# Summing the first quad's exponentials on GpSimd before TensorE takes the softmax sums

## The chip, the cores and the metric

One core of a Trainium2 chip runs the whole kernel. The metric is the device time of one execution in microseconds (us). Engines are named as in the profile: PE is TensorE, PEld its weight loads, DVE is VectorE, ACT is ScalarE, POOL is GpSimd, SP is SyncE.

## The reference

```python
scores = scale * np.matmul(q, k.transpose(0, 1, 3, 2))      # batch 8, 12 heads, 448 rows, head_dim 64
scores = scores - np.max(scores, axis=-1, keepdims=True)
attn = np.exp(scores)
attn = attn / (np.sum(attn, axis=-1, keepdims=True) + 1e-09)
x = (attn @ v)  -> [3584, 768]
h = x @ w_in                                                 # 768 x 2048
out = (h * np.cos(h)) @ w_out                                # 2048 x 768
```

## The kernel before

Four heads make a quad, a batch has three quads (c = 0, 1, 2), and the 448 keys of a quad are handled in seven chunks (r). A planning clock in Python estimates when each engine is free, lays down the order of all instructions ahead of time and gives each engine its own list in that order. The parts that matter:

```python
# S: scores of one chunk on PE, exponential on ACT
nc.scalar.activation(out=pT[b, c][:, r, :, :], in_=sc[:, :, 0:S_], func=AF.Exp, scale=scale)

# DN: sums over keys, on PE, into den (four matmuls, each on 32 columns of its own)
for c in cs:
    for r in rs:                      # seven chunks
        for h in range(2):
            for qh_ in range(2):
                nc.tensor.matmul(den[b][32 * g : 32 * g + 32, :], onehot[:, c, :],
                                 pT[b, c][:, r, h, ts(qh_, SH)], ...)

# N: reciprocal and six small copies on DVE
nc.vector.reciprocal(out=rr[:, 0], in_=den[b])
# ... six copies of 32 rows ...

# M: per quad, two shuffles and one product with two SBUF inputs, on DVE
nc.vector.stream_shuffle(out=rb[:, j], in_=..., mask=[row] * 32)      # j = 0, 1
nc.vector.tensor_tensor(out=xT[b, c], in0=asb[b, c], in1=rb, op=ALU.mult)

# H: the projection to 2048 takes xT quad by quad (hps), then cos on ACT and gT on DVE
# O: the projection back (ops); PE uses it to fill waits in attention and behind den
```

A quad's attention output is copied from PSUM, where this kernel's matmuls put their results, into `asb`; `rb` holds the reciprocals of the sums, spread over the rows by the shuffles; `xT` is their product, the scaled heads. At the end of a batch PE runs `den`, the last `av` and two to five score chunks of the next batch, then `ops` as filler until N and M have made xT.

The softmax here doesn't subtract the row's maximum and nothing guards it: scores larger than these inputs give would overflow.

Of the kernel before, what the change touches and what calls it, by code (L numbers as in the profile page):

```python
# [11 lines left out]
FP = mybir.dt.float32  # L12
F16 = mybir.dt.float16
AF = mybir.ActivationFunctionType
ALU = mybir.AluOpType


class Clock:
# [3 lines left out]


    def __init__(self, slots):
        self.pe = self.act = self.dve = self.stall = 0.0
        self.mode = self.table = None
        self.slots = {k: [0.0] * n for k, n in slots.items()}
        self.ready = {}

    def copy(self):  # L30
        c = Clock({})
        c.pe, c.act, c.dve, c.stall = self.pe, self.act, self.dve, self.stall
        c.mode, c.table = self.mode, self.table
        c.slots = {k: list(v) for k, v in self.slots.items()}
        c.ready = dict(self.ready)
        return c
# [22 lines left out]
    def on_act(self, dep, dur, table=None):  # L59
        if table is not None and table != self.table:  # L60
            self.act += 1.3
            self.table = table
        self.act = max(self.act, dep) + dur
        return self.act + 0.15

    def on_dve(self, dep, dur):
        self.dve = max(self.dve, dep) + dur
# [4 lines left out]
def kernel(  # L72
# [9 lines left out]
    nc = tc.nc  # L82

    B, NH, S_, D = q.shape
    E = moe_w_in.shape[0]
    F = moe_w_in.shape[1]
    P = 128
    NR = 7
    SP = S_ // NR
    NQ = NH // 4  # L90
# [8 lines left out]
    const = ctx.enter_context(tc.tile_pool(name="const", bufs=1))  # L99
    wpool = ctx.enter_context(tc.tile_pool(name="wpool", bufs=1))  # L100
    ld = ctx.enter_context(tc.tile_pool(name="ld", bufs=3))
    sb = ctx.enter_context(tc.tile_pool(name="sb", bufs=2))
    big = ctx.enter_context(tc.tile_pool(name="big", bufs=1))
# [1 line left out]



    clk = Clock({"big": 3, "m": 2, "pT": 4, "qkp": 3, "qkT": 4, "asb": 4, "xT": 3, "gT": 2})


    def quad_rows(t):
# [53 lines left out]

    ident = const.tile([P, P], F16, name="ident")
    onehot = const.tile([P, NQ, 32], F16, name="onehot")
    lowrow = const.tile([P, 1], FP, name="lowrow")
    ind = []
    halfpi = const.tile([P, 1], FP, name="halfpi")  # L170
# [3 lines left out]
    def emit_consts_vector():  # L174
        nc.vector.memset(zero, 0.0)


        nc.vector.memset(onehot, 0.0)
        nc.vector.memset(onehot[:, 0, 2 * NQ : 16], 1.0)
        nc.vector.memset(onehot[:, 0, 16 + 2 * NQ :], 1.0)  # L180
        for j in range(2):
            for half in range(2):
                for c in range(NQ):
                    m = 16 * half + 2 * c + j
                    nc.vector.memset(onehot[64 * j : 64 * j + 64, c, m : m + 1], 1.0)
        nc.vector.memset(halfpi, math.pi / 2)

    def emit_consts_late():

# [25 lines left out]
    pairs, qkT, pT, asb, den, rrs, rhl, xT, gT = ({} for _ in range(9))  # L215
# [151 lines left out]
    def AV(ck, b, c, rs=range(NR)):  # L367
        ck.need(max(ck.ready.get(("pT", b, c, rs[-1]), LATER), arrive["v", b, c]))
        first, last = rs[0] == 0, rs[-1] == NR - 1
        if first:  # L370
            ck.ready["av slot", b, c], t = take(ck, "big", None if b else (2,))
            ck.need(t)
        at = ck.ready["av slot", b, c]
        end = ck.mm("quarters", len(rs), 0.189)
        if last:
            ck.ready["asb slot", b, c], t = take(ck, "asb", None)
            on, took = (ck.on_act, 0.92) if c == NQ - 1 else (ck.on_dve, 1.09)
            ck.slots["big"][at] = ck.ready["asb", b, c] = on(max(end, t), took)
        if ck is not clk:
            return  # L380
        p = pT[b, c]
        vn = nat["v", b, c]
        if first:
            avs[c] = ps.tile([P, 2, 512], FP, name="av", tag=f"big{at}")
        for r in rs:
            for j in range(2):
                for h in range(2):
                    nc.tensor.matmul(  # L388
                        avs[c][64 * h : 64 * h + 64, j, 0:S_],
                        vn[64 * j : 64 * j + 64, h, ts(r, D)],  # L390
                        p[64 * j : 64 * j + 64, r, h, :],
                        start=(r == 0),
                        stop=(r == NR - 1),
                    )
        if not last:
            return
        a = sb.tile([P, 2, S_], FP, name="asb", tag=f"asb{ck.ready['asb slot', b, c]}", bufs=1)
        asb[b, c] = a
        copy = nc.scalar.copy if c == NQ - 1 else nc.vector.tensor_copy
        copy(out=a, in_=avs[c][:, :, 0:S_])  # L400
        emit_load_v()
        if b == 0 and c == 2:
            emit_w_out(1)
            for _ in held_back[1:]:
                emit_load_qk()
            held_back.clear()

    def AVS(ck, b, c, b2, chunks):

        AV(ck, b, c)  # L410
        S(ck, b2, chunks)

    def DN(ck, b, cs, rs=range(NR)):


        ck.need(ck.ready.get(("pT", b, cs[-1], rs[-1]), LATER))
        if cs[0] == rs[0] == 0:
            ck.ready["den slot", b], t = take(ck, "m", None)
            ck.need(t)
        for c in cs:  # L420
            ck.ready["den", b] = end = ck.mm("col32", len(rs), 0.0935)
            if rs[-1] == NR - 1:
                ck.slots["pT"][ck.ready["pT slot", b, c]] = end
        if ck is not clk:
            return
        if cs[0] == rs[0] == 0:
            den[b] = ps.tile([P, SH], FP, name="den", tag=f"m{ck.ready['den slot', b]}")
        for c in cs:
            for r in rs:
                for h in range(2):  # L430
                    for qh_ in range(2):
                        g = 2 * qh_ + h if b < BY_SHUFFLE else 2 * h + qh_
                        nc.tensor.matmul(  # L433
                            den[b][32 * g : 32 * g + 32, :],
                            onehot[:, c, :],
                            pT[b, c][:, r, h, ts(qh_, SH)],
                            start=(c == 0 and r == 0),
                            stop=(c == NQ - 1 and r == NR - 1),
                        )
# [226 lines left out]
    def run(step):  # L666
        step[0](clk, *step[1:])
# [4 lines left out]
    def transpose_ahead():  # L672

        while to_transpose:
            b, c = to_transpose[0]
            now = max(clk.pe, clk.dve)
            if zeros and b > 0:
                return
            if arrive.get(("qk", b, c), LATER) > now - (1.0 if b and c else 0.0) or min(clk.slots["qkp"]) > now or min(clk.slots["qkT"]) > now:
                return  # L680
            to_transpose.pop(0)
            run((W, b, c))
            if (b, c) > BY_PE:
                run((X, b, c))
            else:
                soon.extend([(T, b, c, i) for i in ((0, 1) if b + c == 0 else (1, 0))])

    def weave(lists, keep, late=99):



        body = lists[0]
        while body:
            transpose_ahead()
            waits = []
            todos = ([body, soon] if opening else [soon, body])
            due = stall(body[0]) if opening else 1e9
            for todo in todos + (lists[1:] if len(body) <= late else []):
                while todo and todo[0][0] in (N, M):
                    run(todo.pop(0))  # L700
                if todo:
                    w, took = cost(todo[0])
                    if todo is not body and took > due + 0.15:
                        continue
                    if w <= SLACK:
                        run(todo.pop(0))
                        break
                    waits.append((w, todo))
            else:
                least = min(waits, key=lambda x: x[0])[0] if waits else 1e9  # L710
                if len(fill) > keep or fill and least > 0.3:
                    waits.append((stall(fill[0]), fill))
                    least = min(least, waits[-1][0])
                if zeros and least > 0.15 and due > 0.15:
                    run((Z,))
                elif least > 1e6:
                    clk.pe += 0.1
                else:
                    run(min(waits, key=lambda x: x[0])[1].pop(0))
# [32 lines left out]
    LATER = 1e9  # L752
    SLACK = 0.02
    QUIET = 5
    BY_PE = (2, 0)
    AHEAD, LATE, KEEP = 1, 6, 8
    ctx.enter_context(tc.manual_schedule(engines=None))
# [39 lines left out]
    values = values[:-8] + [step for step in values[-8:] if step[0] is DN] + [(N, 0)] + late  # L797
    last = scores[-QUIET:]
    weave([scores[:-QUIET], values], 0)
    zeros.clear()  # L800
# [4 lines left out]
    body = []  # L805
    for b in range(B):
# [13 lines left out]
        body = ahead + nxt[AHEAD if b else 4 :]  # L820
# [32 lines left out]
```

## Time and profile before

| | before |
|---|---|
| median time | 415.05 us (3 runs, 414.9 to 415.1) |
| span of the profiled run | 413.1 us |
| PE busy, idle | 405.0, 8.1 us |
| POOL busy | 68.6 us, 62.8 of it issuing loads |
| `den` | 672 matmuls, 84 a batch in 2.13 us, 25.4 ns each |
| xT product on DVE | 21 of 1.092 us |

A group's row on the page has the line of code, engine, operation, output and inputs, count, then busy time and mean length of one in ns, then the engine's idle time ahead of the group and what ended most of it. The chain of waits and the order of time give start, length, engine and what. The lines themselves stand in the prediction.

### The profile page before, as it was taken

How to read it: one execution, taken by the hardware profiler on the slowest of the kernel's cores; microseconds unless marked ns; L12 is line 12 of the kernel's file. 1: busy time of each engine (PE TensorE's matmuls, PEld its weight loads, DVE VectorE, ACT ScalarE, POOL GpSimd, SP SyncE). 2: the span in 40 equal slices, each digit the busy share in tenths (PEclk: the TensorE clock that was granted, in tenths of full speed). 3: DMA queues.
4: the chain of work that ended last, by engine and by line, in shares of the span. 5: the costliest groups of instructions: out<-in, count | busy, mean ns of one | idle time of the engine just before them, and what ended most of it. 6: DMA issues, size and time to landing. Idle time of an engine off the chain costs nothing.

```text
span 413.1 us, 8921 instructions
## 1 busy us (share of the span) xinstructions
PE 405.0 (98%) x3835; PEld 217.9 (53%) x3835; DVE 202.7 (49%) x356; ACT 250.2 (61%) x299; POOL 68.6 (17%) x103
## 2 busy tenths in 40 slices
PE   8989999999999999899999999999999999999996
PEld 3445546555565555555565555655556555555564
DVE  3365634945247443754429443575426643294400
ACT  5986386656756478544867457574685547734311
POOL 7687204200320023000230003100000000000000
PEclk9999999999999999999999999999999999999999
DMA  9999999992995039950898009950473101210033
GB/s 191 190 152 201 204 212 200 147 133 63 167 175 108 2 56 174 139 103 2 144 162 146 21 19 110 180 119 2 83 108 78 26 0 40 53 45 2 19 76 79
DMA packets 67239, 42.65 MB, mean 103 GB/s; under 512 B 34304, under 2 KB 67200, under 8 KB 67200
## 3 DMA queue, kind: packets, MB, share of 16 engines
q0 software_dynamic: 26496, 22.35, 38.8%
q1 hardware_dynamic: 40256, 19.18, 26.9%
q8 instruction: 30, 0.49, 0.6%
q10 hardware_dynamic: 448, 0.56, 0.4%
q14 instruction: 9, 0.07, 0.1%
HBM read 45.61 MB, written 11.01 MB: 137 GB/s over the span
## 4 chain that ended last, share of the span: by engine, by line
PE 89%; DMA 4%; DVE 2%; ACT 1%; POOL 1%; issue 1%; POOLq 0%; DVEq 0%
PE ops L635 35%; PE hps L582 34%; PE sc L352 7%; PE av L388 7%; PE den L433 4%; DMA win<-in_moe_w_in_dram 2%; DMA vn<-in_v_dram 2%; DVE rb L482 1%; PE tp L307 1%; ACT pT L361 1%; POOL qkn L133 1%; DVE xT L486 1%; DVE rr L451 0%; POOL vn L143 0%; ACT qkT L319 0%
## 5 line engine op out<-in xcount | busy, mean ns | idle before, releaser
L361 ACT ACTIVATE pT<-sc 128x896 f16<-128x896 f32 x168 | 142.4, 921 | 20.3 <-PE sc L352 20.2
L582 PE MATMUL hps<-xT,win 128*128 128x448 f16 x768 | 149.4, 352 | 0.1
L635 PE MATMUL ops<-wout,gT 128*128 128x384 f16 x768 | 137.5, 327 | 1.3 <-issue 1.3
L592 ACT ACTIVATE cs<-hps,halfpi 128x896 f32<-128x896 f32 x64 | 63.6, 1007 | 79.5 <-PE hps L582 76.7
L582 PEld LDWEIGHTS <-win 128*128 128x128 f16 x768 | 74.8, 98 | 69.2 <-issue 0.9
L593 DVE TENSOR_TENSOR gT<-cs,hps 128x896 f16<-128x896 f32 x64 | 68.9, 1087 | 72.4 <-ACT cs L592 72.3
L635 PEld LDWEIGHTS <-gT 128*128 128x128 f16 x768 | 70.6, 98 | 62.5 <-issue 19.4
L352 PE MATMUL sc<-qkT 64*64 64x448 f16 x672 | 46.9, 357 | 0.7 <-ACT pT L361 0.4
L133 POOL DMA_DIRECT2D qkn<-in_q_dram x23 | 16.6, 722 | 134.4 <-DVE qkp L245 131.3
L388 PE MATMUL av<-pT,vn 64*64 64x448 f16 x672 | 38.0, 353 | 0.3 <-DMA win<-in_moe_w_in_dram 0.3
L400 DVE COPY asb<-av 128x896 f32<-128x896 f32 x16 | 17.5, 1091 | 34.0 <-PE av L388 34.0
L143 POOL DMA_DIRECT2D vn<-in_v_dram x24 | 17.2, 719 | 99.9 <-PE sc L352 98.1
L645 DVE COPY osb<-ops 128x384 f32<-128x384 f32 x25 | 13.9, 556 | 37.2 <-PE ops L635 37.2
L645 ACT COPY osb<-ops 128x384 f32<-128x384 f32 (+1 forms) x32 | 15.1, 472 | 26.6 <-DMA out_dram<-osb 17.0
L352 PEld LDWEIGHTS <-qkT 64*64 64x64 f16 x672 | 17.8, 105 | 22.1 <-issue 15.7
L388 PEld LDWEIGHTS <-vn 64*64 64x64 f16 x672 | 17.7, 106 | 14.9 <-issue 6.5
L482 DVE STREAM_SHUFFLE rb<-rr 128x448 f32<-128x448 f32 x42 | 25.5, 656 | 0.1
L400 ACT COPY asb<-av 128x896 f32<-128x896 f32 x8 | 7.3, 907 | 27.9 <-PE av L388 27.9
L486 DVE TENSOR_TENSOR xT<-asb,rb 128x896 f16<-128x896 f32 x21 | 22.9, 1092 | 1.2
L635 PE MATMUL ops<-wout,rest 128*128 128x384 f16 (+1 forms) x144 | 23.2, 308 | 0.0
L451 DVE RECIPROCAL rr<-den 128x224 f32<-128x224 f32 x8 | 12.5, 1558 | 18.6 <-PE den L433 18.6
L433 PE MATMUL den<-pT,onehot 128*32 128x224 f16 x672 | 18.9, 260 | 0.0
(47 smaller groups left out, 160.7 us busy)
## 6 DMA issues: line engine op xcount, KB each, us to landing
out_dram<-osb SPq DMA_DIRECT2D x110, 96.0 KB, 2.7
vn<-in_v_dram POOLq DMA_DIRECT2D x24, 224.0 KB, 8.1
qkn<-in_q_dram POOLq DMA_DIRECT2D x23, 224.0 KB, 8.0
qkn<-in_k_dram POOLq DMA_DIRECT2D x23, 224.0 KB, 8.8
win<-in_moe_w_in_dram POOLq DMA_DIRECT2D x16, 192.0 KB, 8.4
wout<-in_moe_w_out_dram POOLq DMA_DIRECT2D x2, 1536.0 KB, 18.7
stage<-in_q_dram SPq DMA_DIRECT2D x2, 224.0 KB, 3.6
stage<-in_k_dram ACTq DMA_DIRECT2D x2, 224.0 KB, 3.8
```

The source lines that it names most:

```text
L352: nc.tensor.matmul(sc[lo, h, 0:S_], t[64 * h : 64 * h + 64, 1, r, lo], t[64 * h : 64 * h + 64, 0, :, lo], start=True, stop=True,)
L361: nc.scalar.activation(out=pT[b, c][:, r, :, :], in_=sc[:, :, 0:S_], func=AF.Exp, scale=scale)
L388: nc.tensor.matmul(avs[c][64 * h : 64 * h + 64, j, 0:S_], vn[64 * j : 64 * j + 64, h, ts(r, D)], p[64 * j : 64 * j + 64, r, h, :], start=( ...
L400: copy(out=a, in_=avs[c][:, :, 0:S_])
L433: nc.tensor.matmul(den[b][32 * g : 32 * g + 32, :], onehot[:, c, :], pT[b, c][:, r, h, ts(qh_, SH)], start=(c == 0 and r == 0), stop=(c == ...
L482: nc.vector.stream_shuffle(out=rb[:, j], in_=rrs[b].rearrange("p q s -> p (q s)"), mask=[row] * 32)
L486: nc.vector.tensor_tensor(out=xT[b, c], in0=asb[b, c], in1=rb, op=ALU.mult)
L582: nc.tensor.matmul(hpss[f2][:, i, 0:S_], w_in16[:, kc, ts(2 * f2 + i, P)], xT[b, kc // 2][:, kc % 2, :], start=(kc == 0), stop=(kc == NKC ...
L592: nc.scalar.activation(out=cos, in_=hpss[f2][:, :, 0:S_], func=AF.Sin, bias=halfpi)
L593: nc.vector.tensor_tensor(out=gT[b][:, 2 * f2 : 2 * f2 + 2, :], in0=cos, in1=hpss[f2][:, :, 0:S_], op=ALU.mult,)
L635: nc.tensor.matmul(ops, tokens, w_out16[:, fc, ds(lo, n)], start=(fc == 0), stop=(fc == NFC - 1),)
L645: (nc.scalar.copy if on_act else nc.vector.tensor_copy)(out=osb, in_=ops)
```

## The change

The sums over the seven chunks of quad 0 are first made elementwise on Pool, in FP32. The sum is then split into an FP16 part (ACT, scaled by 1/8) and the FP16 remainder (DVE), written over the first two chunks, and PE sums over partitions with a one-hot of 8. That takes five groups of four matmuls off PE in each of batches 2 to 7. One of four `asb` buffers is given up for the sum's tile. The diff, cut to its core (the planning clock's bookkeeping is left out):

```diff
-    clk = Clock({..., "asb": 4, ...})
+    clk = Clock({..., "asb": 3, ...})
+        nc.vector.tensor_scalar(out=onehot8, in0=onehot, scalar1=8.0, scalar2=None, op0=ALU.mult)
+    SUMMED, SUMMED_FROM = (0,), 2
+    def U(ck, b, c, r):
+        ...
+        if r == 1:
+            totals[b, c] = sb.tile([P, 2, S_], FP, name="sum", tag=f"sum{c}", bufs=1)
+        first = p[:, 0] if r == 1 else totals[b, c]
+        engine = nc.gpsimd if c == 0 else nc.vector
+        engine.tensor_tensor(out=totals[b, c], in0=first, in1=p[:, r], op=ALU.add)
+    def V(ck, b, c):
+        ...
+        nc.scalar.mul(out=hi, in_=totals[b, c], mul=0.125)
+        nc.vector.scalar_tensor_tensor(
+            out=lo, in0=totals[b, c], scalar=0.125, in1=hi, op0=ALU.mult, op1=ALU.subtract)
     def DN(...):
-            for r in rs:
+            for r in range(2) if c in summed else rs:
-                            onehot[:, c, :],
+                            (onehot8 if c in summed else onehot)[:, c, :],
+    def sum_ahead(due):     # emits U and V as soon as the planning clock has their inputs
```

More of the change, by code (lines that the diff above doesn't have):

```diff
@@ L24, in __init__ @@
     def __init__(self, slots):
-        self.pe = self.act = self.dve = self.stall = 0.0
+        self.pe = self.act = self.dve = self.pool = self.stall = 0.0
         self.mode = self.table = None
@@ L31, in copy @@
         c = Clock({})
-        c.pe, c.act, c.dve, c.stall = self.pe, self.act, self.dve, self.stall
+        c.pe, c.act, c.dve, c.pool, c.stall = self.pe, self.act, self.dve, self.pool, self.stall
         c.mode, c.table = self.mode, self.table
@@ L64, in on_act, with on_pool @@
         return self.act + 0.15
+    def on_pool(self, dep, dur):
+        self.pool = max(self.pool, dep) + dur
+        return self.pool + 0.15
     def on_dve(self, dep, dur):
@@ L104 @@
     ps = ctx.enter_context(tc.tile_pool(name="ps", bufs=1, space=bass.MemoryType.PSUM))
-    clk = Clock({"big": 3, "m": 2, "pT": 4, "qkp": 3, "qkT": 4, "asb": 4, "xT": 3, "gT": 2})
+    clk = Clock({"big": 3, "m": 2, "pT": 4, "qkp": 3, "qkT": 4, "asb": 3, "xT": 3, "gT": 2})
     def quad_rows(t):
@@ L167 @@
     onehot = const.tile([P, NQ, 32], F16, name="onehot")
+    onehot8 = const.tile([P, NQ, 32], F16, name="onehot8")
     lowrow = const.tile([P, 1], FP, name="lowrow")
@@ L373, in AV @@
         at = ck.ready["av slot", b, c]
-        end = ck.mm("quarters", len(rs), 0.189)
+        ck.ready["av", b, c] = end = ck.mm("quarters", len(rs), 0.189)
         if last:
@@ L411, in AVS @@
         S(ck, b2, chunks)
+    SUMMED, SUMMED_FROM = (0,), 2
+    totals = {}
+    def U(ck, b, c, r):
+        on, took = (ck.on_pool, 2.1) if c == 0 else (ck.on_dve, 1.0)
+        ck.ready["sum", b, c, r] = on(max(ck.ready["pT", b, c, i] for i in (0, r)), took)
+        if ck is not clk:
+            return
+        p = pT[b, c]
+        if r == 1:
[4 more added lines that the diff above has]
+    def V(ck, b, c):
+        t = ck.on_act(max(ck.ready["sum", b, c, NR - 1], ck.ready["av", b, c]), 0.82)
+        ck.ready["sum", b, c] = ck.on_dve(t, 1.0)
+        if ck is not clk:
+            return
+        hi, lo = (pT[b, c][:, i] for i in range(2))
+        nc.scalar.mul(out=hi, in_=totals[b, c], mul=0.125)
+        nc.vector.scalar_tensor_tensor(
+            out=lo, in0=totals[b, c], scalar=0.125, in1=hi, op0=ALU.mult, op1=ALU.subtract
+        )
     def DN(ck, b, cs, rs=range(NR)):
+        summed = [c for c in cs if b >= SUMMED_FROM and c in SUMMED]
         ck.need(ck.ready.get(("pT", b, cs[-1], rs[-1]), LATER))
+        for c in summed:
+            ck.need(ck.ready.get(("sum", b, c), LATER))
         if cs[0] == rs[0] == 0:
@@ L420, in DN @@
         for c in cs:
-            ck.ready["den", b] = end = ck.mm("col32", len(rs), 0.0935)
+            ck.ready["den", b] = end = ck.mm("col32", 2 if c in summed else len(rs), 0.0935)
             if rs[-1] == NR - 1:
@@ L686, in transpose_ahead @@
                 soon.extend([(T, b, c, i) for i in ((0, 1) if b + c == 0 else (1, 0))])
+    to_sum = {c: [] for c in SUMMED}
+    for b in range(SUMMED_FROM, B):
+        for c in SUMMED:
+            to_sum[c] += [(U, b, c, r) for r in range(1, NR)] + [(V, b, c)]
+    def sum_ahead(due):
+        for c, steps in to_sum.items():
+            while steps:
+                step = steps[0]
+                b = step[1]
+                at = clk.pool if c == 0 and step[0] is U else clk.dve
+                if step[0] is U:
+                    t = clk.ready.get(("pT", b, c, step[3]), LATER)
+                else:
+                    t = max(clk.ready.get(("sum", b, c, NR - 1), LATER), clk.ready.get(("av", b, c), LATER))
+                ready = t <= max(clk.pe, at) and at <= clk.pe + BACKLOG
+                if not ready and b > due:
+                    break
+                run(steps.pop(0))
     def weave(lists, keep, late=99):
@@ L694, in weave @@
             transpose_ahead()
+            sum_ahead(body[0][1] if body[0][0] is DN else -1)
             waits = []
@@ L754 @@
     QUIET = 5
+    BACKLOG = 1.0
     BY_PE = (2, 0)
```

## The prediction

Three things in it are my assumptions, which no trace of the kernel before shows: 2.05 us for a Pool add (the change's planning clock counts 2.1), the whole-instruction rule of case C (an add and an xT product exclude each other for the length of an instruction), and in case B that each xT is stretched by half.

> **What bounds the kernel now.** I read the page first, busy shares and groups, then the chain that ended last, then the instructions in order of time around one batch. On the page of the kernel before:
>
> ```profile
> PE 405.0 (98%) x3835; PEld 217.9 (53%) x3835; DVE 202.7 (49%) x356; ACT 250.2 (61%) x299; POOL 68.6 (17%) x103
> ...
> L486 DVE TENSOR_TENSOR xT<-asb,rb 128x896 f16<-128x896 f32 x21 | 22.9, 1092 | 1.2
> ...
> L433 PE MATMUL den<-pT,onehot 128*32 128x224 f16 x672 | 18.9, 260 | 0.0
> ```
>
> TensorE has work for 98% of the 413.1 us span, so the schedule is a list of PE work with hardly a hole, and an engine that helps is useful only while it makes PE wait for nothing new. The sums over keys (`den`) are 672 matmuls and 18.9 us busy: the only group this change shortens.
>
> The chain of waits, cut to batch 3 (165 to 217 us), shows the price of `den` and the order behind it:
>
> ```profile
> 165.60 2.13 PE den L433 x84
> 167.73 1.45 PE av L388 x28
> 169.18 0.38 PE sc L352 x8
> 169.56 2.38 PE ops L635 x14
> 171.94 0.69 PE sc L352 x12
> 172.63 0.92 PE ops L635 x5
> 173.55 1.26 issue
> 174.81 0.65 PE ops L635 x3
> 175.46 1.51 PE hps L582 x8
> 176.97 0.65 PE ops L635 x4
> 177.62 1.51 PE hps L582 x8
> 179.13 0.65 PE ops L635 x4
> 179.78 15.13 PE hps L582 x80
> ```
>
> After `den`, PE is fed with output matmuls (`ops`) until VectorE has turned den into the scaled heads xT, and the second projection (`hps`) starts on them one quad at a time. In the order of time of DVE and ACT in the same stretch the three xT products and the first exponentials of the next batch stand side by side:
>
> ```profile
> 172.48 1.09 DVE L486 TENSOR_TENSOR xT<-asb,rb 128x896 f16<-128x896 f32 x1
> ...
> 174.73 1.09 DVE L486 TENSOR_TENSOR xT<-asb,rb 128x896 f16<-128x896 f32 x1
> ...
> 177.07 1.09 DVE L486 TENSOR_TENSOR xT<-asb,rb 128x896 f16<-128x896 f32 x1
> ```
>
> ```profile
> 170.03 1.73 ACT L361 ACTIVATE pT<-sc 128x896 f16<-128x896 f32 x2
> ...
> 172.30 2.53 ACT L361 ACTIVATE pT<-sc 128x896 f16<-128x896 f32 x3 [0.17 <-PE sc L352]
> ```
>
> The last xT ends at 177.07 + 1.09 = 178.16 and PE takes up the group that needs it at 179.62 by its own timeline: 1.46 us to spare. I took the same difference in every batch whose successor will be summed on Pool (batches 1 to 6): 0.05, 0.36, 1.46, 0.36, 0.05 and 0.35 us, 2.63 us in all. That is almost nothing: these three products are nearly on PE's path.
>
> [...] The trace before has no Pool arithmetic of this kind. [...] of one of the small copies (rr, L459)
>
> ```profile
> L459 DVE COPY rr<-rr x14: 266/270/331, 74.4 to 365.0; 32x224 f32<-32x224 f32 x14
> ```
>
> the slow ones of 0.33 us are those that ran while Pool was issuing a load of v (169.95 beside the load issued at 169.50); in batch 7, which has no such load, it took 0.27. [...] The trace has 1.092 for xT; I use that for the new subtraction on DVE.
>
> **The change, part by part.** Removed: in batches 2 to 7 quad 0 takes two chunks of four matmuls instead of seven, so 6 x 5 x 4 = 120 matmuls. One group of 84 takes 2.13 us in the chain, 2.13 / 84 = 25.4 ns each[...]. So 120 x 25.4 ns = **3.04 us** of PE, all on the path, 0.73% of 415.05. This is the most the change can win by its own arithmetic.
>
> Added on Pool: 6 batches x 6 adds x 2.05 = 74 us; Pool was busy for 68.6, much of it at the opening, so it has room. In each batch its adds take 12.3 us, and the chance to do them is long: four can follow the exponentials at 170 to 175, two those of the next attention stage (the chunks from 198.4), and the sum is wanted by `den` at 214.97. Even with the two splitting steps it is ready near 207, an estimate from these starts. So den itself won't wait for Pool. Loads issued by Pool can stand behind an add for 2 to 4 us; they take a median 8 us to land and are asked for a quad or more ahead, so I give this nothing.
>
> Added on ACT: six scalings, each about 0.92 us (the asb copy of equal size takes 0.907). ACT is busy for 16.32 of the 20 us from 195 to 215, and its waits there are for PE's scores, so 0.92 fits. Added on DVE: six subtractions of 1.09, in a stage where it's busy for 7.65 of 20. Both wait for finished sums and lie off the path; 0.1 us in all for the one-time scaled one-hot. One asb buffer fewer (3 for 4): its slot is wanted again only after the xT of the batch before, so no wait.
>
> Moved: nothing by hand, but the order is laid by a planning clock, and output matmuls shift among the gaps. I take 0 plus or minus 1 us for it.
>
> **Where it can go wrong: the two engines meet.** [...] The second exponential of the next batch ends at 170.03 + 1.73 = 171.76, so the first add runs from about 171.85 to 173.9. xT 0 wants to start at 172.48, reads two SBUF tensors, and if the whole-instruction rule holds, starts at 173.9 instead (+1.42). It ends at 175.0; the second add then runs to 177.05; xT 1, wanted at 176.16 after its two shuffles, starts at 177.05 (+2.32). The third add runs from 178.14 to 180.19, and xT 2 starts there instead of 177.07 (+3.12). Against 2.63 us of slack over six batches: 6 x 3.12 - 2.63 = 16.1 us of new PE waits, less 3.0 won: +13.1, **428.1 us**.
>
> **The rivals.**
> A: no contention that counts. Then 415.05 - 3.04 with 0.2 lost on the added steps: **412.2 us**. For it: [...] the change is aimed carefully, with start batch and backlog set.
> B: [...] each xT stretched by half: 3 x 0.55 = 1.6 a batch, less 2.63 / 6 = 0.44 slack, x 6 = 7.2, less 3.0: **about 419 us**.
> C: the full lock as worked above, **428.1 us**. For it: [...] the overlap in all six batches. Against it: an add that is faster than 2.05 us shortens it quickly (at 1.6 us the same steps give +1.85 instead of +3.12, near 420).
> D: Pool late, with ACT (in order) held at the scaling, and the exponentials behind it. The window of some 8 us before den speaks against it; at 3 us an add it would begin to bite. I count it within the upper range. If Pool never let DVE in between adds, four adds in a row would cost some 8 us a batch and over 450 us; I give that under 5%.
>
> **Range and chances.** I weigh A 0.35, B 0.20, C 0.45: 0.35 x 412.2 + 0.20 x 419 + 0.45 x 428.1 = 420.7. I put 420.5; it is a mean of unlike outcomes, and the true time is more likely near 412 or above 424 than there. The range, 411.5 to 430, spans A to C. Faster by 2% means under 406.7, 8.3 us won, where 3.04 is the most on the list: 0.01. Slower by 2% is above 423.4: nearly all of C and a little of B, 0.44. The rest, 0.55, is within 2%.
>
> **What the profile after would show.** den x552 matmuls instead of 672 and near 15.5 us busy proves the gain. The mean of one Pool add says whether 2.05 holds. For C the three xT start up to 3 us later behind den than now, with DVE or Pool named between den and `hps` in the chain of waits, in batches 1 to 6 and not in 7; for A the xT keep their distances from den and PE's idle time stays near 8 us. For D, ACT's scaling would wait long for Pool. The prediction is wrong if the planner has moved the adds behind xT, or if the planning clock, with changed costs, lays down a much better or worse order.

## The result, and the profile after

The changed kernel takes **421.67 us** (4 runs, 421.6 to 421.96), the kernel before 414.98 in the same rounds. The ratio is 1.0165, 95% interval 1.0148 to 1.0183: slower, but within 2%. A ratio here is the mean time of one kernel's runs over that of the other's runs of the same rounds, so it isn't quite the ratio of the quoted medians. Executions over 1.5% slower than the fastest of the same kernel are left out of the means.

From the page of the kernel after, the engines' busy shares, the chain by engine, and three groups:

```profile
PE 405.4 (97%) x3715; PEld 214.5 (51%) x3715; DVE 218.0 (52%) x358; ACT 256.0 (61%) x310; POOL 148.4 (35%) x139
...
PE 76%; DVE 19%; ACT 1%; DMA 1%; issue 1%; ACTq 0%; DVEq 0%
...
L620 PE MATMUL hps<-xT,win 128*128 128x448 f16 x768 | 149.4, 353 | 8.3 <-DVE xT L524 8.2
...
L435 POOL TENSOR_TENSOR sum<-sum,pT 128x896 f32<-128x896 f32 x30 | 68.5, 2282 | 36.5 <-ACT pT L367 34.9
...
L524 DVE TENSOR_TENSOR xT<-asb,rb 128x896 f16<-128x896 f32 x21 | 33.1, 1574 | 1.6 <-DVE rb L520 0.5
```

PE's idle time rose from 8.1 to 14.5 us (419.9 - 405.4), and its new idle time lies before `hps` and is ended by xT. The same 21 products take 33.1 us instead of 22.9, though their code is unchanged: 10.2 us more. DVE now makes up 19% of the chain that ends last, where it was 2%.

The expected saving is there, though den is 16.0 us busy and not the 15.5 that were expected. Its group after:

```profile
L471 PE MATMUL den<-pT,onehot 128*32 128x224 f16 x552 | 16.0, 260 | 0.0
```

The chain of waits after, at batch 3, from den to the 80 long matmuls of `hps`:

```profile
168.74 1.67 PE den L471 x64
170.44 1.57 DVE rr L489
...
175.14 2.20 DVE xT L524
...
178.58 1.45 DVE xT L524
...
181.34 1.46 DVE xT L524
182.84 15.29 PE hps L620 x80
```

den is done in 1.67 us instead of 2.13. But where the chain went through PE all the way before, it now goes through DVE: three xT of 2.20, 1.45 and 1.46 us. From the end of den to the end of the third xT it was 178.16 - 167.73 = 10.43 us; now 182.80 - 170.41 = 12.39. The order of time of the same stretch shows who lies beside them:

```profile
174.58 1.87 POOL L435 TENSOR_TENSOR sum<-pT 128x896 f32<-128x896 f16 x1 [1.71 <-ACT pT L367]
175.14 2.26 DVE L524 TENSOR_TENSOR xT<-asb,rb 128x896 f16<-128x896 f32 x1
176.53 8.00 POOL L435 TENSOR_TENSOR sum<-sum,pT 128x896 f32<-128x896 f32 x3
...
177.33 0.65 DVE L520 STREAM_SHUFFLE rb<-rr 128x448 f32<-128x448 f32 x1
...
178.58 1.51 DVE L524 TENSOR_TENSOR xT<-asb,rb 128x896 f16<-128x896 f32 x1
...
181.34 1.45 DVE L524 TENSOR_TENSOR xT<-asb,rb 128x896 f16<-128x896 f32 x1
```

The two engines take turns. The first add ends at 174.58 + 1.87 = 176.45; the xT that wanted to start at 175.14 ends at 177.40, 0.95 us later. The second add, recorded from 176.53, is stretched in its turn: the three take 8.00 us with the gaps between them, some 2.6 each, against 1.87 for the first, which held the product up. The shuffles between the products have one SBUF input; they lie beside the same adds and keep their 0.65 us. Note how the profile shows the wait: the product blocked at 175.14 has no idle time ahead of it and no releaser. It only looks longer than its kind.

### The profile page after: what moved, and what is told of

It reads as the page before. It is cut to its first block, busy times and chain, and to the rows that moved or that the text cites. A ratio compares the mean times of both kernels' runs of the same rounds, so it can differ in the third digit from the quotient of the medians.

```text
span 419.9 us, 8770 instructions
## 1 busy us (share of the span) xinstructions
PE 405.4 (97%) x3715; PEld 214.5 (51%) x3715; DVE 218.0 (52%) x358; ACT 256.0 (61%) x310; POOL 148.4 (35%) x139
## 4 chain that ended last, share of the span: by engine, by line
PE 76%; DVE 19%; ACT 1%; DMA 1%; issue 1%; ACTq 0%; DVEq 0%
PE hps L620 30%; PE ops L673 27%; DVE xT L524 7%; PE sc L358 7%; DVE rb L520 6%; PE av L394 6%; PE den L471 4%; DVE rr L489 3%; PE tp L313 1%; DVE rr L497 1%; DMA stage<-in_k_dram 1%; DVE rr L496 1%; PE z L237 1%; DVE rr L495 1%; ACT pT L367 1%
## 5 line engine op out<-in xcount | busy, mean ns | idle before, releaser
L620 PE MATMUL hps<-xT,win 128*128 128x448 f16 x768 | 149.4, 353 | 8.3 <-DVE xT L524 8.2
L435 POOL TENSOR_TENSOR sum<-sum,pT 128x896 f32<-128x896 f32 x30 | 68.5, 2282 | 36.5 <-ACT pT L367 34.9
L524 DVE TENSOR_TENSOR xT<-asb,rb 128x896 f16<-128x896 f32 x21 | 33.1, 1574 | 1.6 <-DVE rb L520 0.5
L683 ACT COPY osb<-ops 128x384 f32<-128x384 f32 (+1 forms) x37 | 17.7, 477 | 24.9 <-DMA out_dram<-osb 12.8
L444 DVE SCALAR_TENSOR_TENSOR pT<-sum,pT 128x896 f16<-128x896 f32 x6 | 6.6, 1092 | 27.1 <-ACT pT L443 27.1
```

The lines of the kernel that those rows point to most:

```text
L435: engine.tensor_tensor(out=totals[b, c], in0=first, in1=p[:, r], op=ALU.add)
L620: nc.tensor.matmul(hpss[f2][:, i, 0:S_], w_in16[:, kc, ts(2 * f2 + i, P)], xT[b, kc // 2][:, kc % 2, :], start=(kc == 0), stop=(kc == NKC ...
```

## The experiments

Theory **L**: a Pool add and a DVE instruction with two SBUF inputs exclude each other for the length of an instruction, which makes xT late and PE wait. Rival **O**: the changed order of PE's work costs the time. Rival **S**: the split on ACT and DVE does.

### The adds held back behind xT

```diff
         if r == 1:
             totals[b, c] = sb.tile([P, 2, S_], FP, name="sum", ...)
+            nc.vector.memset(totals[b, c][:, 0, 0:1], 0.0)     # behind the third xT of batch b-1
```

The planning clock is told of the same wait, so that it emits the add only once xT is due. The memset of one column lies behind the third xT on DVE's list, and the add that overwrites the tile waits for it.

> The changed kernel, but each batch's first Pool add also waits, through a one-element VectorE memset of the sum's tile placed behind the third xT product of the batch before, until the three xT products are done. Correct result. Theory L (a Pool add and a VectorE product with two SBUF inputs exclude each other for a whole instruction, and the late xT makes PE wait): all 21 xT back to 1.09 us, Pool adds all near 1.88 us, PE's waits for xT gone; time of the kernel before less 6 x 0.45 us of den = about 412.3 (412 to 413.2). Rival O (the changed order of PE's work costs the time): the order is nearly that of the changed kernel, so 419 to 422. Rival S (the split on ACT and VectorE costs): 419 or more, xT at 1.09 all the same.

It is correct and takes 412.11 us (4 runs, 411.89 to 415.98; before 415.19, ratio 0.9954, interval 0.9907 to 1.0000, wide because of one run of 415.98). The order of time in this kernel:

```profile
177.21 1.09 DVE L526 TENSOR_TENSOR xT<-asb,rb 128x896 f16<-128x896 f32 x1
...
181.39 0.06 DVE L434 MEMSET sum<- 128x1 f32 x1
181.65 1.87 POOL L437 TENSOR_TENSOR sum<-pT 128x896 f32<-128x896 f16 x1 [11.30 <-DVE sum L434]
183.38 1.09 DVE L633 TENSOR_TENSOR gT<-cs,hps 128x896 f16<-128x896 f32 x1 [0.93 <-ACT cs L632]
183.60 5.82 POOL L437 TENSOR_TENSOR sum<-sum,pT 128x896 f32<-128x896 f32 x3
```

xT is back at 1.09, and the adds are at 1.87 to 1.95. The gT product at 183.38 lies beside adds without being lengthened, as do the next two (185.65 and 187.92, 1.09 us each, beside adds up to 189.42): of its inputs, `cs` is in SBUF and `hps` in PSUM. So it isn't any DVE arithmetic that collides, and moving the adds removes the whole loss with all of the change's other work still in place. The traces of this run and of the changed kernel have PE's 3715 matmuls in the same order, group by group. O and S both fall.

### The adds taken away, the order kept

```diff
-        engine.tensor_tensor(out=totals[b, c], in0=first, in1=p[:, r], op=ALU.add)
```

The tile of the sum is a constant here, set once early, so the result is wrong; den's two chunks and the split stay.

> The changed kernel in the same order with the 36 Pool adds taken away; the sums are a constant tile, so the result is wrong on purpose; den keeps its two chunks and the split on ACT and VectorE stays. Theory L: 412 to 413, xT 1.09 us. Rivals O and S: both order and split are still there, so near 421.

412.19 us (412.02 to 413.14), ratio 0.9938 (0.9918 to 0.9958), all xT at 1.092. The changed order (again the same on PE, group by group) and the split, still present, cost nothing that can be seen, and the saving without a price is 0.6%. The held version, with its adds, is as fast as one without any.

### The adds without the saving

```diff
-            for r in range(2) if c in summed else rs:
+            for r in rs:
-                            (onehot8 if c in summed else onehot)[:, c, :],
+                            onehot[:, c, :],
-        # the two splitting instructions of V removed
```

> The Pool adds without the saving: den takes all seven chunks again, the sums are made and not used, and there is no split. Correct result. Theory L: the price of the adds alone on top of the kernel before. From the changed kernel (421.7) plus the 6 x 0.45 us of den that it saves: 424 to 425, mean xT 1.57 us as in the changed kernel. If the split on ACT and VectorE carried a price of its own, this would come out below 423.

Correct, 424.78 us (424.51 to 425.09; before 414.53, of whose seven runs one of 421.29 is slow and not in the ratio), ratio 1.0255 (1.0232 to 1.0277). From its page:

```profile
L519 DVE TENSOR_TENSOR xT<-asb,rb 128x896 f16<-128x896 f32 x21 | 33.5, 1594 | 1.2
```

The adds alone cost 424.78 - 414.53 = 10.2 us, with den at its old size and no split. The longer products are 33.5 - 22.9 = 10.6 us. The change is thus the sum of two parts: some 10 us lost by the adds, some 3 won by den (424.78 - 421.67 = 3.1).

### Read side or write side

```diff
-        engine.tensor_tensor(out=totals[b, c], in0=first, in1=p[:, r], op=ALU.add)
+        engine.tensor_copy(out=peek, in_=p[:, r, 0, 0:1])      # waits for the same exponential
+        for _ in range(2):
+            engine.memset(totals[b, c], 64.0)                  # writes, reads nothing
```

> The changed kernel with each Pool add replaced by a one-column copy that waits for the same exponential and two memsets of the sum's tile, which write SBUF and read nothing; the result is wrong on purpose. If the meeting place is the read side: xT back to 1.09 us (up to 1.2 where a one-column copy falls on it) and 412 to 413.5, though Pool is as busy in the same stretch. If any Pool work on SBUF locks VectorE out, or the writes meet: xT 1.4 us or more and 418 to 422.

Three runs took 412.02 to 413.06 us and one 826.39, and the profile fell on that one: its `hps` matmuls had a mean of 621 ns against 352 and were busy for 318.9 us against 149.4, at a granted clock recorded as 1.0, while ACT (exponentials of 917 ns against 921) and DVE (xT at 1.09 us) kept their speed. Its cause is open. That run isn't used. The ratio is 0.9938 (0.9914 to 0.9961).

> The kernel of the write-only run again, for a profile in the fast state: the first profile fell on a run in which TensorE was twice as slow throughout (826 us, the other three 412 to 413). Read side as the meeting place: all xT 1.09 us though Pool's memsets lie beside them, and 412 to 413.5 us. Otherwise xT above 1.3 us in batches 1 to 6.

412.06 us; of a single run the state is unknown, but the time agrees with the fast runs. Pool's order of time in it, then DVE's:

```profile
171.93 1.74 POOL L438 MEMSET sum<- 128x896 f32 x2
...
175.80 1.74 POOL L438 MEMSET sum<- 128x896 f32 x2
177.49 0.71 POOL L436 CAST peek<-pT 128x1 f32<-128x1 f16 x1
```

```profile
172.46 1.09 DVE L527 TENSOR_TENSOR xT<-asb,rb 128x896 f16<-128x896 f32 x1
...
177.07 1.09 DVE L527 TENSOR_TENSOR xT<-asb,rb 128x896 f16<-128x896 f32 x1
```

Pool is busy in the same stretch as with adds, and the first memsets (171.93 to 173.67) lie over the first xT, which still takes 1.09. These writes don't collide with it. A read does even with one column: the copy at 177.49 takes 0.71 us where the two beside no xT (171.81 and 173.62) take 0.18, and it ends at 178.20, just after the third xT (178.16).

### The adds cut in half

```diff
-        engine.tensor_tensor(out=totals[b, c], in0=first, in1=p[:, r], op=ALU.add)
+        for h in range(2):
+            engine.tensor_tensor(
+                out=totals[b, c][:, h], in0=first[:, h], in1=p[:, r, h], op=ALU.add)
```

> The changed kernel with each Pool add cut into two instructions of 448 columns. Correct result. Theory L with exclusion for a whole instruction: an xT now waits for at most about 1 us of a half add instead of up to 1.9, so the mean xT falls from 1.57 to some 1.3 us and the time to 416 to 419. If exclusion is finer than an instruction [...], halving changes nothing: mean xT 1.5 to 1.6, 421 to 423.

This missed in neither of the ways I had named: 427.41 us (426.47 to 428.27), ratio 1.0307 (1.0283 to 1.0331), slower still. The order of time in batch 1, Pool and then DVE:

```profile
81.30 2.03 POOL L436 TENSOR_TENSOR sum<-pT 128x448 f32<-128x448 f16 x2
83.28 5.96 POOL L436 TENSOR_TENSOR sum<-sum,pT 128x448 f32<-128x448 f32 x6
```

```profile
82.22 7.97 DVE L527 TENSOR_TENSOR xT<-asb,rb 128x896 f16<-128x896 f32 x1
```

Eight half adds ran through at about 1 us each without a break, and the xT waited for all of them, 7.97 us; so the wait isn't always bounded by one instruction. In the later batches the two took turns, at 1.41, 1.65 and 1.59 us in batch 3. Just behind the long wait PE was also granted less clock, 0.92 on average from 90.2 to 107 us, where it is 1.00 from 107 on; the 80 `hps` matmuls took 16.58 us there against 15.29. To see if this one event was all, I held back the first adds alone:

> The half adds again, with the first adds (those of batch 2, beside the xT of batch 1) alone held back behind the third xT by a two-element memset; the later batches as in the run of halves. Correct result. The halves run cost 427.4 us, and in its profile one xT of batch 1 lasts 7.97 us beside eight half adds in a row. If that one event (some 7 us, and the slower stretch of TensorE just after it) is what the halves lost, this comes to 416 to 420; if halves are worse in every batch, 424 or more.

418.35 us (418.25 to 418.83), ratio 1.0092 (1.0071 to 1.0113). From its page:

```profile
L529 DVE TENSOR_TENSOR xT<-asb,rb 128x896 f16<-128x896 f32 x21 | 29.8, 1418 | 1.2
```

So the halves do shorten the collisions (1418 ns against 1574, though in this run batch 1 has none at all, which flatters it; in batch 3 the three products grow by 1.38 us against 1.94), and the loss of the first run was, for the most part, the one starved product and its aftermath. Why Pool did not let DVE in during that run of adds, and did in later batches, isn't settled. In batch 1 all the inputs were long there, as Pool had been behind two load issues until 81.3. That alone doesn't explain it: in the changed kernel Pool is behind the same issues until 81.35, and there the third xT of batch 1 got in after one add. What else differs is that each add of the changed kernel needs the one before, and starts 0.08 us after it ends, while halves of different columns don't need each other. I didn't test whether that matters.

### One buffer fewer, alone

```diff
-    clk = Clock({..., "asb": 4, ...})       # in the kernel before
+    clk = Clock({..., "asb": 3, ...})
```

> The kernel before with three asb buffers in place of four, nothing else. All theories of mine: within 0.3 us of the kernel before. If the missing buffer costs something, 416 or more with waits for asb.

414.92 us (414.17 to 415.22) against 414.53, ratio 1.0012 (0.9992 to 1.0033): no difference.

### Further versions of the held kernel

The first sums quad 1 as well, on DVE, in the same tile once quad 0 is split:

```diff
-    SUMMED, SUMMED_FROM = (0,), 2
+    SUMMED, SUMMED_FROM = (0, 1), 2        # one sum tile for both, quad 1 waits for quad 0's split
```

> The held version with quad 1 summed too, by VectorE, in the same sum tile after quad 0 is split. Correct result. Another 6 x 0.45 us of den leave PE: 409.5 if VectorE's six more adds and the split (some 7.7 us a batch) find room; 412 or more if they make copies out of PSUM late or den wait for the last sum.

It is correct and takes 445.51 us (444.8 to 446.39), ratio 1.0754 (1.073 to 1.0779). In its waits:

```profile
PE ops L676 <- ACT osb L686: 20.0, 6, 4.2
```

On ACT's list the scaling of the second sum stands ahead of the copies that free PE's output buffers, and it waits for the last DVE add: in batch 2 the add ends at 121.82, the scaling starts at 121.85 after 3.67 us of idle time, and the copies at 122.70. PE waits behind those copies for up to 4.2 us a batch. This is my rival D of the prediction, in a kernel where the sum is late; in the changed kernel it doesn't occur. The 20.0 us of waits are most of the 31 us lost; the granted clock was lower too (0.972), and I didn't take the rest apart.

The second starts the sums in batch 1; the third is the held version again, with more rounds.

```diff
-    SUMMED, SUMMED_FROM = (0,), 2
+    SUMMED, SUMMED_FROM = (0,), 1
```

> The held version with the sums starting in batch 1 in place of batch 2. In batch 0 the scaled heads come from another path, whose products read PSUM. Correct result. One more 0.45 us of den saved: 411.6 to 412.0 if Pool has room between its loads in batch 1; 413 or more if the adds push loads of batch 2 or ACT's scaling back.

> The held version once more, for a narrower interval (one of its four runs was 415.98 us, the others 411.9 to 412.3). Theory L: 412.0 to 412.4, ratio to the kernel before 0.993 to 0.995.

From batch 1: 412.51 us (411.93 to 413.45), ratio 0.9953 (0.9936 to 0.9969); the seventh batch gains nothing that can be seen. The held version: **411.95 us** (5 runs, 411.91 to 412.23; before 414.67), ratio 0.9939 (0.9924 to 0.9955). It is faster than both kernels.

## Why the prediction was right or wrong

The time lay inside the range and in the class given most weight, and the mechanism of rival C was the true one, though B's number, 419, lies nearer to the result than C's 428.1. The point, 420.5, came close for a poor reason: it was the mean of unlike cases, and the prediction's own remark that the truth would rather be near 412 or above 424 than near that mean was wrong. Step by step:

- **What is removed** was right: 120 matmuls fewer, 3.04 us predicted. By the chain it is 6 x (2.13 - 1.68) = 2.7 us, where most batches show den at 1.68; by the runs 2.7 to 3.1. The sum for rival A, 412.2, is what the run without adds took (412.19).
- **What is added off the path** was right: sums came in time, ACT's scaling and DVE's subtraction cost nothing visible (the run without adds), and neither did the buffer (its own run).
- **The meeting of Pool and DVE** was right in kind: named instructions, named batches, turn by turn. Batch 7, with no successor, indeed kept its xT at 1.09. Rival A (no contention, weight 0.35) fell; the 60 ns by which a small copy of the trace before was longer (0.33 us against 0.27) were of one with one SBUF input beside a load's issue, which is as long in the changed kernel (0.33) and says nothing of two inputs. B as a mechanism (each xT stretched all through the overlap) fell too: in batch 3 each of the three products ends 0.94 or 0.95 us after the end of an add, and halved adds shorten the wait.
- **Its size was too large: 16.1 us predicted, 9.5 to 10.2 measured.** Three terms of the delay were off. An add takes 1.88 us, not 2.05. A product that waited ends some 0.95 us after the add instead of 1.09, as if its start were already behind it. With both, my own steps give 2.2 us at the third xT; measured in batch 3 it is 12.39 - 10.43 = 1.96 rather than 3.12. And in batch 1 the adds stood behind load issues until 81.35, so that only the third xT was hit (1.92 us long, 0.83 more). In batches 1 to 6 the third xT ends 0.84, 1.96, 1.97, 1.97, 1.97 and 1.90 us later behind den than before, 10.6 in all, not 6 x 3.12 = 18.7. (The aside that an add of 1.6 us would give +1.85 has a slip: the same steps give +1.76. Nothing rests on it.)
- **The slack was too generous.** I took 2.63 us from the kernel before, 1.46 of it in batch 3, where PE has a hole of 1.26 us ("issue" in its chain). The changed order has no such hole. In the held version, with PE's order that of the changed kernel, the third xT ends 0.05, 0.36, 0.05, 0.36, 0.05 and 0.36 us before PE takes up its group: 1.23 in all. And a PE that waited starts 0.05 us behind the xT, 0.3 in six batches. Then 10.6 - 1.2 + 0.3 = 9.7 us; the changed kernel less the held one is 421.67 - 411.95 = 9.7. Less 2.7 for den, that is 7.0 against the kernel before; measured 421.67 - 414.98 = 6.7.
- **A trap in reading PE.** The 80 `hps` matmuls take 15.13 us in the chain before and 15.29 after, but that is no cost: in the order of time they take 15.30 and 15.29. The record of a group overlaps the one before by some 0.15 us, which the chain leaves out, and after a wait there is nothing to overlap. So PE's idle time, 6.4 us more, shows only a part of the 9.7.
- **Never letting DVE in**, which I gave under 5%, doesn't happen in the changed kernel, but did once in the halves.

## What to carry to other kernels

An idle engine isn't free if its instructions can hold up those of the engine on the critical path: look for instructions of the two with SBUF inputs at the same time (here xT took up to 2.26 us beside Pool adds, and 1.09 without them), and let the helper's work start behind the critical ones. A one-column write to the helper's tile, placed behind the critical instruction, was enough to hold it (0.06 us), and turned 1.7% lost into 0.6% won. In a profile, suspect such a collision where an unchanged instruction of one of the two got longer beside the other's, without any wait ahead of it.
